# One low part ahead of the first row gather's index, one gate gathered two steps sooner, and each subtraction bound ahead of the next maxima

## The chip, the cores and the metric

The kernel runs on one core of a Trainium2 chip. The metric is the device time of one execution in microseconds (us); lower is better. Five engines work side by side, each on its own queue in order: TensorE (PE, with its weight loads shown apart as PEld), VectorE (DVE), ScalarE (ACT), GpSimd (POOL) and SyncE (SP, which here only issues transfers). They wait for each other through semaphores.

## What is computed

A linear attention over 8 batches, 8 heads, 576 positions and 64 channels, and behind it a mixture of 8 experts in which every token goes to its best expert alone:

```python
def phi(x):
    proj = np.einsum('bhsd,df->bhsf', x, w_phi)            # 64 -> 128 features
    proj = proj - np.max(np.abs(proj), axis=-1, keepdims=True)
    return np.concatenate([np.exp(proj), np.exp(-proj)], axis=-1)
q_p, k_p = phi(q), phi(k)
kv  = np.einsum('bhsf,bhsd->bhfd', k_p, v)
num = np.einsum('bhsf,bhfd->bhsd', q_p, kv)
den = np.einsum('bhsf,bhf->bhs', q_p, k_p.sum(2))[..., None] + 1e-6
x   = (num / den) as rows of 4608 tokens x 512
...
expert = argmax(x @ w_gate)                                # 8 experts
out[token] = gate[token] * (relu(x[token] @ w1[expert]) @ w2[expert])   # 512 -> 1024 -> 512
```

## The kernel before

**Attention.** It runs in 16 units of two batches and two heads. A unit's k and q are cut into pieces of one or two chunks of 128 positions (named by their first chunk: k8, k0, k2, ...). `project` multiplies a piece by w_phi into a PSUM tile `ps_proj` (two of them in turn), VectorE takes the maxima of the absolute values (L320) and subtracts them (L321, which is the last reader of `ps_proj`), ScalarE takes the two exponentials. Outside the first unit every fp32 factor is split in a high part (rounded copy, by ScalarE) and a low part (the rest, by VectorE or GpSimd), and a product is three matmuls. Then come the products with v (`pk`), a fold with w_gate, and the numerators (`pn`). The order of TensorE's work is written out by `half`, `PLAN_A` and `PLAN_B`; that of the other engines is set by a scheduler, except where `behind(m, other)` binds m after another instruction of its own engine, without a semaphore, or `paced(m, other)` makes m wait for an instruction of another engine. The first unit's loads and pieces stand in the string `ORDER`: `Lk2` loads part 2 of k, `VLt` the tail of v, `k4` projects piece 4.

**Routing.** Each token's place among its expert's tokens becomes a block of 128 rows. `tokens_of` multiplies selections into `pp`; VectorE turns it into `gidx`, the rows to gather for each block (L1030), `sidx`, the rows to write to, and `rows_f`. `experts_of` compares block numbers with the experts' bounds (`eg`, four instructions of L1065), GpSimd finishes `eg` (L1072, L1073) and VectorE sums it to `eidx`, the expert of each block (L1075), which SyncE reads to load weights.

**Experts.** Blocks are worked in 19 pairs, u = 0 to 18, and then one by one. Of each pair, `pair_first` makes the hidden layer (L1192 to L1194: products of high by high, low of x by high, high by low of the weights), ScalarE its relu's high part `hh` (L1199), VectorE the low part `hl` (L1200); `pair_second` multiplies by w2 (L1212 to L1214, of which L1214 needs `hl`). Both run over j = 0 to 3. `weights(u, k)` splits piece k of a pair's weights: `wh` by ScalarE (L1109), `wl` by VectorE (L1110). Pieces k = 4 to 7 are w2's. Pair 0's weights serve pair 1 too. `x_parts` turns the gathered rows `xg` of a block into `xh` and `xl` (with TensorE in pairs 0 and 1, L1173; later with VectorE, L1166). `write` scales a finished block by its gate on ScalarE (`ob`, L1267) and GpSimd scatters it (L1269).

Gathers run on GpSimd, in order: rows by `gidx` for block 3 (blocks 0 to 2 were gathered ahead), and from pair 2 on rows in quarters by `qidx`, eight to a pair; gates (`gate`) by `gather_gates`. The pair loop issues, at each j, a part of the quarters of pair u + 2, and at j = 3 the gates of pair u.

Of the kernel before, what the change touches and what calls it, by code (L numbers as in the profile page):

```python
# [9 lines left out]
F32 = mybir.dt.float32  # L10
# [4 lines left out]
ALU = mybir.AluOpType  # L15
# [41 lines left out]
def tile_linear_attention_moe(  # L57
# [144 lines left out]

    ORDER = "Lk0 Lk1 VLt Lk2 VL0 Lq0 k8 Lq1 Nk0 VL1 Lq2 Vt k0 V0 k2 C V1 k4 W"

# [83 lines left out]
    def chain(m):  # L288
# [3 lines left out]
        behind_order[0] = m  # L292

    def project(st, x, c0, n, link=lambda m: None):

# [16 lines left out]
        if st["u"] == 0 and (x, c0) == ("k", 4):  # L312
# [6 lines left out]
        psv = ps[:, 0:n].rearrange("p i h f -> p (i h) f")  # L319
        V.tensor_reduce(mx[:, 0 : 2 * n], psv, axis=AX.X, op=ALU.max, apply_absolute_value=True)  # L320
        V.tensor_tensor(  # L321
            t[:, 0 : 2 * n, :],
# [579 lines left out]
    def fetch_rows(out, source, index, rows):  # L902
        m = G.indirect_dma_start(  # L903
            out=out,
            out_offset=None,
            in_=source[0:rows],
            in_offset=bass.IndirectOffsetOnAxis(ap=index, axis=0),
            bounds_check=rows - 1,
            oob_is_err=False,
        )  # L910
        if lining[0]:
            lined(m)
        return m

# [83 lines left out]
    def block_of():  # L998
# [17 lines left out]
        for j0 in range(0, NTILE, 12):  # L1016
            V.tensor_tensor(
                bsel[:, j0 : j0 + 12, :],
                iota_p[:, 0:NB].unsqueeze(1).to_broadcast([P, 12, NB]),
                bi[:, j0 : j0 + 12].unsqueeze(2).to_broadcast([P, 12, NB]),  # L1020
                op=ALU.is_equal,
            )
# [33 lines left out]
    def experts_of():  # L1056
# [6 lines left out]
        for low, high, n0, n1 in places:  # L1063
            for j, edge in enumerate((low, high)):
# [5 lines left out]
                )  # L1070
                behind(m, st["places"])
        G.tensor_tensor(eg[:, 0], eg[:, 0], eg[:, 1], op=ALU.subtract)  # L1072
        st["experts"] = G.tensor_tensor(eg[:, 0], eg[:, 0], iota_e[0:1].unsqueeze(1).to_broadcast([1, NB, E]), op=ALU.mult)  # L1073
# [24 lines left out]
    def weights(u, k):  # L1098
# [12 lines left out]
        if (u, k) == (0, KD + 3):  # L1111
            behind(m, st["places"])
        for j in range(2) if u == 0 else [u]:
# [211 lines left out]
    tokens_of()  # L1325
    gather(1)
    weights(0, KD + 3)
    pair_second(0, 1)
# [17 lines left out]
    for u in range(1, NPAIR):  # L1346
# [5 lines left out]
        for j in range(4):  # L1352
            pair_first(u, j)
            for f in (parts[0], parts[2], parts[3], ())[j]:
                f(st["step"])
            if j == 3:
                for f in extra:
                    f(st["step"])
            if j in (1, 2):
# [116 lines left out]
```

## Time and profile before

| what | value |
|---|---|
| time, median of 3 runs | 868.35 us (868.28 to 869.65) |
| profiled execution, own time | 867.14 us |
| its span, first to last instruction | 865.3 us |
| granted TensorE clock, mean | 0.999 of full speed |
| busy share PE / PEld / DVE / ACT / POOL | 99 / 93 / 73 / 66 / 66 % |

The span is the part of the profiled execution in which instructions ran; 1.84 us of its own time lie outside. The profiled execution was 1.21 us shorter than the median of the runs. A matmul's end is modelled, so a short wait of TensorE shows fully only in its weight loads (PEld).

### The profile page before, as it was taken

How to read it: one execution, taken by the hardware profiler on the slowest of the kernel's cores; microseconds unless marked ns; L12 is line 12 of the kernel's file. 1: busy time of each engine (PE TensorE's matmuls, PEld its weight loads, DVE VectorE, ACT ScalarE, POOL GpSimd, SP SyncE). 2: the span in 40 equal slices, each digit the busy share in tenths (PEclk: the TensorE clock that was granted, in tenths of full speed). 3: DMA queues.
4: the chain of work that ended last, by engine and by line, in shares of the span. 5: the costliest groups of instructions: out<-in, count | busy, mean ns of one | idle time of the engine just before them, and what ended most of it. 6: DMA issues, size and time to landing. Idle time of an engine off the chain costs nothing. (4 is left out here: it accounts for less than half of the span.)

```text
span 865.3 us, 18092 instructions
## 1 busy us (share of the span) xinstructions
PE 855.6 (99%) x6589; PEld 803.8 (93%) x6589; DVE 634.9 (73%) x1049; ACT 570.9 (66%) x880; POOL 567.0 (66%) x419
## 2 busy tenths in 40 slices
PE   9999999999999999999999999999999999999997
PEld 7999999999999999999889999999999999999985
DVE  7678778887888788949768666666666777676672
ACT  6888888888778887753646555555555555555572
POOL 5667666876677767663887666666666666664772
PEclk9999999999999999999999999999999999999999
DMA  6233333523343334261154243541535644445651
GB/s 208 86 103 96 106 105 103 101 83 113 114 114 108 107 105 94 62 225 30 50 182 138 70 145 121 161 122 47 164 111 165 230 125 139 144 128 192 221 171 40
DMA packets 69884, 106.65 MB, mean 123 GB/s; under 512 B 13918, under 2 KB 31838, under 8 KB 69792
## 3 DMA queue, kind: packets, MB, share of 16 engines
q1 hardware_dynamic: 59312, 84.50, 32.7%
q0 software_dynamic: 9808, 20.81, 7.8%
q8 instruction: 53, 0.87, 0.4%
q14 instruction: 39, 0.32, 0.1%
q10 hardware_dynamic: 672, 0.15, 0.1%
HBM read 128.42 MB, written 20.26 MB: 172 GB/s over the span
## 5 line engine op out<-in xcount | busy, mean ns | idle before, releaser
L1110 DVE TENSOR_TENSOR wl<-raw,wh 128x1024 fp32r<-128x1024 f32 x160 | 201.5, 1270 | 91.1 <-ACT wh L1109 87.7
L903 POOL DMA_INDIRECT xg<-x_dram,qidx x148 | 174.4, 1179 | 76.2 <-ACT hh L1199 36.1
L1109 ACT CAST wh<-raw 128x1024 fp32r<-128x1024 f32 x168 | 174.4, 1047 | 40.0 <-PE po L1214 20.8
L490 PE MATMUL pn<-kf,qp 128*128 128x73 f32 (+1 forms) x1152 | 184.8, 255 | 0.0
L1194 PE MATMUL pm<-xh,wl 128*128 128x256 f32 x608 | 172.2, 283 | 0.0
L1193 PE MATMUL pm<-xl,wh 128*128 128x256 f32 x608 | 172.1, 283 | 0.0
L490 PEld LDWEIGHTS pn<-kf,qp 128*128 128x128 f32 x1152 | 171.4, 189 | 0.5
L1192 PE MATMUL pm<-xh,wh 128*128 128x256 f32 x608 | 171.6, 282 | 0.0
L355 POOL TENSOR_TENSOR kl<-e,kh 128x1024 fp32r<-128x1024 f32 x45 | 107.5, 2388 | 97.8 <-ACT kh L353 97.8
L320 DVE TENSOR_REDUCE mx<-ps_proj 128x4 f32<-128x512 f32 (+1 forms) x159 | 100.3, 632 | 49.3 <-PE ps_proj L310 48.2
L1213 PE MATMUL po<-wl,hh 128*128 128x512 f32 x304 | 119.3, 392 | 0.0
L1212 PE MATMUL po<-wh,hh 128*128 128x512 f32 x304 | 119.2, 393 | 0.0
L1214 PE MATMUL po<-wh,hl 128*128 128x512 f32 x304 | 118.3, 390 | 0.7 <-DVE hl L1200 0.7
L1192 PEld LDWEIGHTS pm<-xh,wh 128*128 128x128 f32 x608 | 116.4, 191 | 2.8
L1193 PEld LDWEIGHTS pm<-xl,wh 128*128 128x128 f32 x608 | 116.4, 191 | 2.8
L1194 PEld LDWEIGHTS pm<-xh,wl 128*128 128x128 f32 x608 | 116.4, 191 | 0.1
L321 DVE TENSOR_TENSOR t<-ps_proj,mx 128x512 f32<-128x512 f32 (+1 forms) x159 | 100.5, 634 | 4.4
L256 POOL TENSOR_TENSOR xl<-xr,xh 128x640 fp32r<-128x640 f32 (+1 forms) x60 | 96.8, 1630 | 9.4 <-ACT xh L255 8.8
L420 PE MATMUL pk<-kh,vl 128*64 128x256 f32 x300 | 101.1, 337 | 0.0
L420 PE MATMUL pk<-kl,vh 128*65 128x256 f32 x300 | 99.6, 332 | 0.0
L420 PE MATMUL pk<-kh,vh 128*65 128x256 f32 x300 | 99.2, 331 | 0.0
L903 POOL DMA_INDIRECT gate<-g_dram,gidx x41 | 58.2, 1418 | 54.8 <-ACT hh L1199 47.6
(223 smaller groups left out, 1889.4 us busy)
## 6 DMA issues: line engine op xcount, KB each, us to landing
raw<-w SPq DMA_DIRECT2D x168, 512.0 KB
vt<-vv SPq DMA_DIRECT2D x15, 640.0 KB
x_dram<-xrow SPq DMA_DIRECT2D x30, 256.0 KB
xr<-kT SPq DMA_DIRECT2D x15, 320.0 KB
xr<-qT SPq DMA_DIRECT2D x15, 320.0 KB
xr<-kT SPq DMA_DIRECT2D x17, 256.0 KB
xr<-qT SPq DMA_DIRECT2D x17, 256.0 KB
xg<-x_dram,qidx POOLq DMA_INDIRECT x148, 3.2
```

What stands on the lines that cost most here:

```text
L355: eng.tensor_tensor(kl, e[:, 0:m], kh, op=ALU.subtract)
L420: return T.matmul(st["pk", bb][0:n, hh, :], (vl if j == 1 else vh)[:, 2 * (c + (bb if c == 8 else 0)) + hh, 0:n], (kl if j == 2 else kh)[: ...
L490: m = T.matmul(pn[:, i - a, :] if c < 8 else pn[:, 2 + hh : 6 : 2, :], qp[:, s, s0 + hh, :], st["kf"][:, hh, s, c // 4, :] if c < 8 else s ...
L903: m = G.indirect_dma_start(out=out, out_offset=None, in_=source[0:rows], in_offset=bass.IndirectOffsetOnAxis(ap=index, axis=0), bounds_che ...
L1109: A.copy(th, raw[k])
L1110: m = (G if k in (POOL_LO0 if u == 0 else POOL_LO if u >= NPAIR else ()) else V).tensor_tensor(tl, raw[k], th, op=ALU.subtract)
L1192: T.matmul(pm[:, i], th, xh[:, k, :], start=(k == 0), stop=False)
L1193: T.matmul(pm[:, i], th, xl[:, k, :], start=False, stop=False)
L1194: T.matmul(pm[:, i], tl, xh[:, k, :], start=False, stop=(k == KD - 1))
L1212: T.matmul(po, hh[:, i, r], th[:, c], start=(i == j == 0), stop=False)
L1213: T.matmul(po, hh[:, i, r], tl[:, c], start=False, stop=False)
L1214: T.matmul(po, hl[:, i, r], th[:, c], start=False, stop=(i == 1 and j == 3))
```

## The change

Five edits:

- `ORDER`: the load of part 2 of k moves ahead of the load of v's tail (`Lk2` ahead of `VLt`).
- `project`: outside the first unit each L320 is bound behind the L321 of the piece before it.
- `weights(0, 7)`: its low part `wl`, bound behind the last instruction for `sidx` before, is bound behind `bsel`, which stands ahead of `gidx`.
- After `gather(1)` (the gather of block 3) GpSimd sets a tile `sent`, and the four `eg` instructions of VectorE wait for it.
- In pair 1 the gate (of block 3; the other is gathered already) is issued at j = 1 ahead of that step's quarters, not at j = 3. For other pairs nothing moves.

```diff
-    ORDER = "Lk0 Lk1 VLt Lk2 VL0 Lq0 k8 ..."
+    ORDER = "Lk0 Lk1 Lk2 VLt VL0 Lq0 k8 ..."
@@ project
-        V.tensor_reduce(mx[:, 0 : 2 * n], psv, axis=AX.X, op=ALU.max, apply_absolute_value=True)
-        V.tensor_tensor(
+        m = V.tensor_reduce(mx[:, 0 : 2 * n], psv, axis=AX.X, op=ALU.max, apply_absolute_value=True)
+        if shifted[0] is not None and st["u"] > 0:
+            behind(m, shifted[0])
+        shifted[0] = V.tensor_tensor(
@@ fetch_rows
+        st["fetch"] = m
@@ block_of
-            V.tensor_tensor(
+            st["bsel"] = V.tensor_tensor(
@@ experts_of
                 behind(m, st["places"])
+                paced(m, st["sent"])
@@ weights
         if (u, k) == (0, KD + 3):
-            behind(m, st["places"])
+            behind(m, st["bsel"])
@@
     gather(1)
+    st["sent"] = G.memset(sg.tile([1, 1], F32, name="sent"), 0.0)
+    behind(st["sent"], st["fetch"])
@@ pair loop
             pair_first(u, j)
+            if j == (1 if u == 1 else 3):
+                for f in extra:
+                    f(st["step"])
             for f in (parts[0], parts[2], parts[3], ())[j]:
                 f(st["step"])
-            if j == 3:
-                for f in extra:
-                    f(st["step"])
```

VectorE at a boundary between two units of the attention, before: the maxima (`mx`) and the subtraction (`t`) of a narrow piece, k8 (128x2 maxima, 128x256 elements), and of the wide piece behind it. The line numbers of the changed kernel are some lines higher.

```order
L355 TENSOR_TENSOR kl<-e,kh 128x1024
L320 TENSOR_REDUCE mx<-ps_proj 128x2
L320 TENSOR_REDUCE mx<-ps_proj 128x4
L321 TENSOR_TENSOR t<-ps_proj,mx 128x256
L321 TENSOR_TENSOR t<-ps_proj,mx 128x512
```

The same place on VectorE now:

```order
L359 TENSOR_TENSOR kl<-e,kh 128x1024
L322 TENSOR_REDUCE mx<-ps_proj 128x2
L325 TENSOR_TENSOR t<-ps_proj,mx 128x256
L322 TENSOR_REDUCE mx<-ps_proj 128x4
L325 TENSOR_TENSOR t<-ps_proj,mx 128x512
```

The narrow piece's subtraction now stands ahead of the wide piece's maxima. The two orders differ so at three unit boundaries and once at the end of the first unit; everywhere else they already stood as now.

VectorE around the index of block 3's gather, before (`wl` is the low part of `weights(0, 7)`; behind the last row, in both kernels, come the other three `eg`, `qidx`, an `xl`, `eidx`, and the `xl` of block 3):

```order
L1017 TENSOR_TENSOR bsel<-iota_p,bi 128x528 x3
L1030 TENSOR_SCALAR gidx<-pp 128x44
L1032 TENSOR_SCALAR emp<-pp 128x44
L1033 SCALAR_TENSOR_TENSOR sidx<-pp,emp 128x44
L1035 TENSOR_SCALAR rows_f<-pp 128x44
L1110 TENSOR_TENSOR wl<-raw_5836,wh 128x1024
L1065 TENSOR_TENSOR eg<-iota_p,first 1x304
```

The same place on VectorE now:

```order
L1022 TENSOR_TENSOR bsel<-iota_p,bi 128x528 x3
L1116 TENSOR_TENSOR wl<-raw_5836,wh 128x1024
L1035 TENSOR_SCALAR gidx<-pp 128x44
L1037 TENSOR_SCALAR emp<-pp 128x44
L1038 SCALAR_TENSOR_TENSOR sidx<-pp,emp 128x44
L1040 TENSOR_SCALAR rows_f<-pp 128x44
L1070 TENSOR_TENSOR eg<-iota_p,first 1x304
```

`wl` moved from behind the four instructions that read `pp` to ahead of them; the rest kept its order. On TensorE two products L1192 stood ahead of the first L1193 of pair 1 before, and one stands there now.

GpSimd from the end of routing into pairs 1 and 2, before (`out` is the scatter of a finished block; rows of quarters are run together):

```order
L1073 TENSOR_TENSOR eg<-eg,iota_p 1x352
L903 DMA xg<-x_dram,qidx 128x128 x8
L1269 DMA out<-ob,sidx_74 4608x512
L903 DMA xg<-x_dram,qidx 128x128 x2
L1269 DMA out<-ob,sidx_74 4608x512
L903 DMA xg<-x_dram,qidx 128x128 x6
L903 DMA gate<-g_dram,gidx 128x4
```

The same place on GpSimd now:

```order
L1079 TENSOR_TENSOR eg<-eg,iota_p 1x352
L907 DMA xg<-x_dram,qidx 128x128 x8
L1275 DMA out<-ob,sidx_74 4608x512
L907 DMA xg<-x_dram,qidx 128x128 x2
L1275 DMA out<-ob,sidx_74 4608x512
L907 DMA xg<-x_dram,qidx 128x128
L907 DMA gate<-g_dram,gidx 128x4
L907 DMA xg<-x_dram,qidx 128x128 x7
```

The gate passes five quarters; each of these five is sent one instruction later.

## Rows read from the trace of the kernel before

**Rows 1.** The page, part 1: busy us of each engine, share of the span, instructions.

```profile
PE 855.6 (99%) x6589; PEld 803.8 (93%) x6589; DVE 634.9 (73%) x1049; ACT 570.9 (66%) x880; POOL 567.0 (66%) x419
```

**Rows 2.** Busy time by stretch: the stretch and its length in us, busy us of each engine with its instructions, granted clock, DMA share, GB/s.

```profile
0.00:10.00 10.00, 8.84 (x34) 5.72 (x35) 6.55 (x20) 4.45 (x8) 4.66 (x22) 1.00 0.80 255
500.00:700.00 200.00, 200.00 (x1288) 182.75 (x1287) 136.08 (x143) 112.66 (x143) 124.95 (x107) 1.00 0.44 139
```

**Rows 3.** The waits of TensorE's weight loads: who waited, for whom, us in total, times, longest.

```profile
PEld px L1173 <- DMA xg<-x_dram,gidx: 1.8, 1, 1.8
PEld po L1214 <- DVE hl L1200: 1.2, 1, 1.2
PEld ps_proj L305 <- DMA xr<-kT: 0.9, 2, 0.7
```

**Rows 4.** The timeline of the first 9 us: start us, us, engine (SPq issues transfers), what, in brackets the idle time before and who ended it. The transfer at 2.21 is part 2 of k, that at 1.73 the tail of v; L305 projects, L407 copies v beside a column of ones, L432 is the first product with v.

```profile
1.73 0.44 SPq L400 DMA_DIRECT2D vt<-vv  x1
2.21 0.43 SPq L246 DMA_DIRECT2D xr<-kT  x1
6.42 0.73 PEld L305 LDWEIGHTS ps_proj<-w_bd,xr 128*128 128x128 f32 x4 [0.71 <-DMA xr<-kT]
5.39 0.40 POOL L407 COPY vf<-vt 128x256 f32<-128x256 f32 x1 [3.38 <-DMA vt<-vv]
7.39 0.59 PE L432 MATMUL pk<-ef,vf 128*65 128x256 f32 x2
```

**Rows 5.** The timeline at the three unit boundaries where TensorE's weight loads wait; VectorE and ScalarE at the first of them.

```profile
147.52 1.01 DVE L320 TENSOR_REDUCE mx<-ps_proj 128x2 f32<-128x256 f32 x2
148.45 1.01 DVE L321 TENSOR_TENSOR t<-ps_proj,mx 128x256 f32<-128x256 f32 x2
148.17 0.58 ACT L452 COPY kvT<-pk 65x512 f32<-65x512 f32 x1 [1.57 <-PE pk L420]
148.98 0.19 PEld L308 LDWEIGHTS ps_proj<-w_hi,xh 128*128 128x128 f32 x1 [0.23 <-ACT kvT L452]
243.40 0.19 PEld L308 LDWEIGHTS ps_proj<-w_hi,xh 128*128 128x128 f32 x1 [0.26 <-ACT kvT L452]
337.85 0.19 PEld L308 LDWEIGHTS ps_proj<-w_hi,xh 128*128 128x128 f32 x1 [0.27 <-ACT kvT L452]
```

**Rows 6.** The timeline around the gather of block 3 and the products that wait for it.

```profile
400.00 1.04 ACT L1109 CAST wh<-raw 128x1024 fp32r<-128x1024 f32 x1
407.94 1.95 DVE L1017 TENSOR_TENSOR bsel<-iota_p,bi 128x528 bf16<-128x528 f32 x3
410.73 0.20 DVE L1030 TENSOR_SCALAR gidx<-pp 128x44 int32<-128x44 f32 x1 [0.85 <-PE pp L1029]
411.31 1.22 DVE L1110 TENSOR_TENSOR wl<-raw,wh 128x1024 fp32r<-128x1024 f32 x1
411.45 2.00 POOL L903 DMA_INDIRECT xg<-x_dram,gidx  x1 [6.56 <-DVE rows_f L1035]
412.44 0.46 DVE L1065 TENSOR_TENSOR eg<-iota_p,first 1x304 f32<-1x304 f32 x1
415.57 0.51 DVE L1075 TENSOR_REDUCE eidx<-eg 1x44 int32<-1x352 f32 x1 [1.14 <-POOL eg L1073]
415.85 0.75 PE L1173 MATMUL px<-ident,xg 128*128 128x128 f32 x4 [1.41 <-DMA xg<-x_dram,gidx]
416.64 0.59 ACT L1174 CAST xh<-px 128x512 fp32r<-128x512 f32 x1 [2.96 <-PE px L1173]
417.25 0.69 DVE L1175 TENSOR_TENSOR xl<-px,xh 128x512 fp32r<-128x512 f32 x1 [1.18 <-ACT xh L1174]
417.82 0.40 PE L1192 MATMUL pm<-xh,wh 128*128 128x256 f32 x2
418.06 0.33 PE L1193 MATMUL pm<-xl,wh 128*128 128x256 f32 x1
```

**Rows 7.** Two other gathers on GpSimd: VectorE's work beside the one, GpSimd's next instruction behind the other.

```profile
427.85 3.49 DVE L1110 TENSOR_TENSOR wl<-raw,wh 128x1024 fp32r<-128x1024 f32 x3
430.28 1.98 POOL L903 DMA_INDIRECT xg<-x_dram,qidx  x1 [0.30 <-ACT hh L1199]
373.20 2.38 POOL L355 TENSOR_TENSOR kl<-e,kh 128x1024 fp32r<-128x1024 f32 x1
372.19 0.99 POOL L903 DMA_INDIRECT xg<-x_dram,gidx  x1 [0.30 <-issue]
```

**Rows 8.** The timeline around the gate of block 3, up to TensorE's wait for `hl`; the first row is the fourth quarter of pair 3's rows, the last the transpose of pair 3's second block.

```profile
437.01 1.00 POOL L903 DMA_INDIRECT xg<-x_dram,qidx  x1 [0.30 <-DVE wl L1110]
444.73 1.00 POOL L903 DMA_INDIRECT gate<-g_dram,gidx  x1 [0.30 <-issue]
448.40 0.69 ACT L1267 ACTIVATE ob<-po,gate 128x512 f32<-128x512 f32 x1 [4.97 <-DMA gate<-g_dram,gidx]
450.06 2.36 DVE L1110 TENSOR_TENSOR wl<-raw,wh 128x1024 fp32r<-128x1024 f32 x2 [7.38 <-ACT wh L1109]
452.33 0.68 DVE L1200 SCALAR_TENSOR_TENSOR hl<-pm,hh 128x512 fp32r<-128x512 f32 x1
453.07 0.50 PE L1214 MATMUL po<-wh,hl 128*128 128x512 f32 x1 [0.73 <-DVE hl L1200]
457.38 1.13 DVE L1166 STREAM_TRANSPOSE px<-xg 128x512 f32<-128x512 f32 x1
```

More of the change, by code (lines that the diff above doesn't have):

```diff
@@ L198, in raw_view @@
         return raw[k].rearrange("p (c f) -> p c f", c=2)
-    ORDER = "Lk0 Lk1 VLt Lk2 VL0 Lq0 k8 Lq1 Nk0 VL1 Lq2 Vt k0 V0 k2 C V1 k4 W"
+    ORDER = "Lk0 Lk1 Lk2 VLt VL0 Lq0 k8 Lq1 Nk0 VL1 Lq2 Vt k0 V0 k2 C V1 k4 W"
     V0 = {"t": (16, 20), "0": (0, 8), "1": (8, 16)}
@@ L292, in chain @@
         behind_order[0] = m
+    shifted = [None]
     def project(st, x, c0, n, link=lambda m: None):
```

## The prediction

> **What bounds the kernel now.** I read the busy time first: TensorE is busy for 855.6 of 865.3 us [rows 1], and from 500 to 700 us without a gap, at full granted clock [rows 2]. So the kernel ends when TensorE has done its list. An edit that takes work or waits from another engine gives nothing, unless TensorE waited for it, and then it gives what TensorE waited. Next I read the waits of TensorE's weight loads, since the ends of its products are modelled and hide short waits. There are few: 1.8 us for the gather of block 3, 1.2 for `hl`, 0.9 for transfers of k, 0.7 of it in one wait [rows 3], and three of 0.23 to 0.27 us that are put down to `kvT` [rows 5]. TensorE also waits at the very start and behind its last product, which the change does not touch. Last I read the timeline at each of these places, and set the five edits beside them. Each place has an edit, so the sum is over the places.
>
> **A. Part 2 of k ahead of v's tail.** SyncE issues v's tail at 1.73 and part 2 of k at 2.21 [rows 4]. The weight loads for piece 4 come at 6.42, after 0.71 idle that a transfer of k ended. Moved, that transfer is issued 0.48 us earlier, and 128 KB of v no longer lie ahead of it. In a stretch that moves 255 GB/s [rows 2] those would be 0.5 us. The gain is then about 0.5. It is bounded below by 0.3, where the transfer gains little, above by the whole wait, 0.71. The cover to watch is v's tail, which now comes later: its copy ran from 5.39 to 5.79, and the first product with v starts at 7.39 [rows 4], with 1.6 us between. In its new place the tail should have landed when part 2 of k had, at about 6.3. A copy of 0.40 ends at 6.7, against a product wanted at 6.9. I take **-0.5**.
>
> **B. Subtractions ahead of the next maxima.** TensorE's L308 projects into a `ps_proj` that the narrow piece's L321 must have read. At the first boundary both maxima run from 147.52 to 148.53, and only then the two subtractions, from 148.45 [rows 5]. The narrow one takes about 0.42 of these 1.01 us and ends at 148.87; the weight load goes at 148.98, 0.11 later. `kvT`, to which the profile gives the wait, had ended at 148.75, and a projection does not read it. Now the narrow subtraction follows the narrow maxima, which end at about 147.94. It ends at about 148.4, before TensorE wants the place at 148.75. The three waits, 0.23 + 0.26 + 0.27, go: **-0.75**. The wide piece's subtraction ends as before, since the same four instructions stand in the same stretch. The fourth place, at the end of the first unit, shows no wait: 0 by itself, but its earlier subtraction frees its `ps_proj` for a TensorE that A has made earlier.
>
> **C. `wl` ahead of `gidx`, and `sent`.** Before, `gidx` starts at 410.73, the gather at 411.45 (0.72 later), and it takes 2.00 us, until 413.45. The rows land 2.40 us behind that, when L1173 starts at 415.85 [rows 6]. VectorE was idle for 0.85 ahead of `gidx`, and `wl`'s `wh` is ScalarE's work of 400.00 to 401.04, so `wl` can start when `bsel` ends, at 409.89, and ends at 411.11. `gidx` goes from 410.73 to 411.11, a loss of 0.38, and the gather starts at 411.83. Does it still take 2.00? Another gather, started at 430.28 beside `wl` instructions that end at 431.34, ends at 432.26, 0.92 behind them; ours ended 0.92 behind its `wl` (412.53). One without `wl` beside it takes 0.99 [rows 7]. So I take 1.0: it ends at 412.83, 0.62 earlier, and the rows land at 415.23.
>
> [...]
>
> `sent` costs something. The `eg` instructions wait for a tile set behind the gather, so they start at about 413.0, not at 412.44: +0.56. From there to the end of `eidx` (416.08) are 3.64 us through GpSimd and back, so `eidx` ends at 416.64. Behind it on VectorE stands block 3's `xl`, which L1193 needs at 418.06. Its other input, `xh`, ends 0.62 earlier, at 416.61. `xl` so starts at 416.65 and not at 417.25, and L1193 at 417.46. Of these 0.60, 0.12 go back, as only one L1192 (0.12 each, 417.82 to 418.06 for two) fills the time ahead of it. Behind `eidx` also wait SyncE's weight loads and GpSimd's quarters for pair 2, 0.56 later. Pair 1 has yet to run, with 96 products of 0.12 and 48 of twice the columns, some 20 us by this estimate, so I cost that at nothing. `rows_f` comes 0.4 later to TensorE, ahead of the long wait that swallows it. L1193 comes 0.2 earlier if the gather takes 1.3, 0.5 if it takes 1.0: **-0.4**.
>
> **D. The gate of block 3.** ScalarE stood for 4.97 us until 448.40 for this gate, which GpSimd sent at 444.73, behind eight quarters [rows 8]. Behind it in ScalarE's queue were two `wh`, so VectorE stood 7.38 us, and then ran two `wl` (450.06 to 452.42) ahead of `hl`, which L1214 wanted. TensorE lost 0.73 by its products, 1.2 by its weight loads. Now the gate takes the turn of the fourth quarter, sent at 437.01. With C's 0.56 it goes at about 437.6 and, with the 3.7 us that the old one took (444.73 to 448.40), lands at 441.3. ScalarE wants it at 443.43. Even 3 us later the two `wl` would be done before `hl` is due. The five quarters it passes belong to pair 3 and go 1.3 us later (1.00 and 0.30 of issue). The last of them was sent before the gate, and VectorE's transpose of that block is at 457.38, without a wait, so I cost that at nothing. I take **-1.0**, between 0.73 and 1.2.
>
> **The sum.** 0.5 + 0.75 + 0.4 + 1.0 = 2.65 us, all of it waits of TensorE, with nothing else late in its list. Against the profiled execution's own 867.14 that is 864.5. That execution lay 1.21 under the median of the runs, 868.35, so for the median I forecast **865.7 us**, 0.3% faster.
>
> **The rivals.**
>
> 1. *v's tail lands late.* The copy of v then holds the first product with v, and A is lost: -2.15, 866.2 us. For it: the margin is only 0.2 us. Against: the same bytes are moved by the same moment as before.
> 2. *The gather keeps its 2.00 us.* It starts 0.38 later, ends at 413.83, and `eg` starts at 413.95. `eidx` ends at 417.6, `xl` at 418.3, L1193 comes at 418.4, and with the L1192 that is gone C is +0.46: -1.8, 866.55 us. Against: [rows 7].
> 3. *The boundary waits are for `kvT`, as the profile says.* B is nothing: -1.9, 866.45 us. Against: 0.23 us between its end and the weight load, where the subtraction's end fits to 0.11.
> 4. *The waits change place.* TensorE, earlier by each gain, runs into the next late thing (a load of k, weights that come by their own pace), and the end stays: 868.35 us. For it: behind every wait stands a second input that was not timed, as `eidx` in C. Against: 200 us on end in which TensorE never waits [rows 2].
> 5. *Slower: `sent` is set only when the gathered rows have landed.* Place: VectorE's queue ahead of `eidx`. The gather starts at 411.83; with the 4.40 us that it took to land, `eg` would start at 416.2, `xl` at 419.85, L1193 at 420.7, which is +2.6, or +2.7 with the L1192. Against -2.25 elsewhere the kernel is 0.45 slower, 868.8 us. It decides from a landing about 3.9 us behind the start, and each us more costs one. Against: behind a gather of 0.99 us GpSimd's next instruction started 0.02 later [rows 7].
>
> **How the numbers follow.** About 0.2%, 1.7 us, is what a measurement of this kernel can tell from no change. Chances: forecast 0.63, rivals 0.10, 0.10, 0.05, 0.08 and 0.04. The bounds of the terms add up to 1.98 to 3.17, or 866.4 to 865.2. The rest of the range is what executions differ by: one here lay 1.2 under the median, so I go down to 864.5. Upward it takes in rivals 1 to 3 with 0.7 for that spread, to 867.3. Faster by over 0.2% is below 866.6: nearly all of the forecast (0.60) and about six in ten of rivals 1 to 3 (0.15), together 0.75. Slower by over 0.2% is rival 5 with a late landing and what I have not thought of, 0.05; the rest, 0.20, is within.
>
> **What would show it.** A: the weight loads of piece 4 without a wait, at about 5.8. B: no wait of L308 at the three boundaries, each narrow subtraction right behind its maxima. C: a gather of about 1.0 us, the first L1173 wait at most 1.3 us. D: no `ob` held for a gate in pair 2's start, no wait of L1214. The forecast is wrong if one of these waits stays, if the first product with v waits for its copy, or if L1193 waits for `xl` behind `eidx` longer than before.

## The result: slower, by a stall that no term of the forecast held

The changed kernel takes **875.9 us** (median of 6 executions, 875.14 to 877.32) where the kernel before, run beside it, takes 868.56 (868.28 to 870.01): ratio 1.0083, 95% interval 1.007 to 1.0096. The forecast was 865.7, so the prediction was wrong in sign.

The profiled execution took 875.14 us, its span 873.1. The page after, busy time and granted clock in 40 slices of 21.8 us, against [rows 1]:

```profile
PE 860.1 (99%) x6589; PEld 806.4 (92%) x6589; DVE 635.6 (73%) x1049; ACT 570.9 (65%) x880; POOL 564.2 (65%) x420
PEclk9999999999999999999899999999999999999999
```

One slice has a lower clock, the twentieth. Busy time by stretch (columns as in [rows 2]):

```profile
400.00:420.00 20.00, 19.46 (x176) 16.77 (x175) 15.54 (x43) 6.29 (x9) 8.51 (x11) 1.00 0.09 22
420.00:440.00 20.00, 15.16 (x73) 12.07 (x72) 8.00 (x9) 8.10 (x10) 13.71 (x13) 0.83 0.20 60
440.00:460.00 20.00, 19.63 (x130) 17.84 (x129) 19.12 (x21) 13.45 (x18) 12.67 (x10) 1.00 0.60 188
500.00:700.00 200.00, 200.00 (x1279) 182.33 (x1278) 136.99 (x144) 110.87 (x142) 125.21 (x107) 1.00 0.45 141
```

The same stretch of the kernel before:

```profile
420.00:440.00 20.00, 20.00 (x137) 18.53 (x136) 19.34 (x21) 15.41 (x19) 16.34 (x13) 1.00 0.35 111
```

From 420 to 440 us, in pair 1, TensorE starts 73 products where it started 137, and VectorE and ScalarE do half of what they did. DMA is not the cause that meets the eye: its share is 0.20, less than before. Before and after that stretch the kernel runs as foreseen; from 500 to 700 TensorE is busy without a gap, as in [rows 2].

Since TensorE has the same 6589 products in both kernels, the n-th can be set beside the n-th. This table (worked out from the traces) gives by how many us a product starts later (+) or earlier (-) than in the kernel before, less that difference at the 20th product, at 7 us. The columns x2 to x16 are experiments below.

| product that starts before at | changed | x2: no C | x7: C without `sent` | x6: C without `wl` | x16: no gathers of pair 2 |
|---|---|---|---|---|---|
| 147.7 us (ahead of the first boundary) | +0.22 | -0.01 | 0.00 | +0.19 | +0.20 |
| 339.0 (behind the third) | -0.40 | -0.99 | -0.98 | -0.43 | -0.42 |
| 410.1 (ahead of C's place) | -0.29 | -0.94 | -0.93 | -0.33 | -0.33 |
| 421.6 (behind it) | -0.88 | -0.89 | -1.36 | -0.28 | -0.89 |
| 443.6 (ahead of D's place) | **+8.80** | -0.89 | -1.37 | -0.28 | -0.89 |
| 459.9 (behind it) | +7.80 | -1.89 | -2.36 | -1.28 | -1.88 |

So the edits gained most of what they were to gain (1.88 us in x16), and in the changed kernel about 9.7 us were lost between 421 and 444.

**The stall.** TensorE's waits there have no releaser; the profile puts them down to "issue" (the two largest groups; who waited, for whom, us in total, times, longest):

```profile
PE pm L1198 <- issue: 1.9, 2, 1.0
PE pm L1200 <- issue: 1.8, 3, 1.0
```

The timeline of the changed kernel there (L907 gathers, L1275 scatters, L1205 is `hh`, L1206 `hl`, L1116 `wl`; the rows of each engine by themselves, TensorE's last):

```profile
415.80 1.04 POOL L907 DMA_INDIRECT xg<-x_dram,qidx  x1 [0.16 <-issue]
...
419.75 1.03 POOL L907 DMA_INDIRECT xg<-x_dram,qidx  x1 [0.30 <-issue]
421.09 1.00 POOL L907 DMA_INDIRECT xg<-x_dram,qidx  x1 [0.30 <-issue]
...
431.60 1.03 POOL L907 DMA_INDIRECT xg<-x_dram,qidx  x1 [0.31 <-issue]
435.57 1.00 POOL L907 DMA_INDIRECT gate<-g_dram,gidx  x1 [2.94 <-ACT hh L1205]
...
422.09 0.60 ACT L1205 ACTIVATE hh<-pm 128x512 fp32r<-128x512 f32 x1 [2.50 <-remote]
434.39 0.60 ACT L1205 ACTIVATE hh<-pm 128x512 fp32r<-128x512 f32 x1 [9.81 <-remote]
...
419.82 1.22 DVE L1116 TENSOR_TENSOR wl<-raw,wh 128x1024 fp32r<-128x1024 f32 x1
435.02 0.69 DVE L1206 SCALAR_TENSOR_TENSOR hl<-pm,hh 128x512 fp32r<-128x512 f32 x1 [10.07 <-ACT hh L1205]
...
419.74 0.28 PE L1200 MATMUL pm<-xh,wl 128*128 128x256 f32 x1
428.50 0.28 PE L1200 MATMUL pm<-xh,wl 128*128 128x256 f32 x1 [1.01 <-issue]
```

GpSimd alone runs freely: thirteen indirect DMAs from 415.80 to 432.63, each about 1.0 us with 0.30 between. ScalarE's second `hh` waits 9.81 us for products that TensorE had started by 422.6; it goes at 434.39, 1.8 us behind the end of GpSimd's run. VectorE waits for that `hh`, and TensorE, which has work that waits for nobody, starts a product every 0.7 us or so instead of every 0.12. It stands idle for 4.84 of the 20 us, and from 431, behind the first of these gaps, to 437 it is granted a clock of 0.50 of full speed, where it has 1.00 up to 430 and from 438 on (0.83 over the stretch). The kernel before, at the same place of the program:

```profile
420.94 1.97 POOL L903 DMA_INDIRECT xg<-x_dram,qidx  x1 [0.31 <-issue]
423.22 1.50 POOL L903 DMA_INDIRECT xg<-x_dram,qidx  x1 [0.30 <-issue]
...
420.82 1.22 DVE L1110 TENSOR_TENSOR wl<-raw,wh 128x1024 fp32r<-128x1024 f32 x1
421.06 0.60 ACT L1199 ACTIVATE hh<-pm 128x512 fp32r<-128x512 f32 x1 [0.46 <-PE pm L1194]
```

There the fifth gather began 0.12 us *into* a `wl` and was stretched to 1.97, the next to 1.50, and no `hh` was late. In the changed kernel the edits have brought TensorE, ScalarE and VectorE 0.9 to 1.0 us forward in pair 1 (0.6 of it C's, by the table) but the quarters back by 0.11 (415.80, not 415.69): the fourth gather starts 0.07 us *ahead* of the `wl`, takes 1.03, and the fifth finds VectorE idle.

The lost stretch is not how the stall begins, though. The last product that the first `hh` needs starts at 419.74 and ends at 420.02. In x16, which has no stall, that `hh` follows this product's end by 0.04. Here it was due at about 420.06, with the fourth gather under way, and it came 2.0 late; the fifth gather began only at 421.09.

The places of the four edits in the changed kernel, in the order A, B, C, D (against [rows 4], [rows 5], [rows 6] and [rows 8]):

```profile
2.21 0.91 SPq L404 DMA_DIRECT2D vt<-vv  x2
6.42 0.73 PEld L307 LDWEIGHTS ps_proj<-w_bd,xr 128*128 128x128 f32 x4 [0.65 <-DMA xr<-kT]
6.89 0.40 POOL L411 COPY vf<-vt 128x256 f32<-128x256 f32 x1 [4.88 <-DMA vt<-vv]
7.34 0.19 PEld L436 LDWEIGHTS pk<-ef,vf 128*65 128x65 f32 x2 [0.20 <-POOL vf L411]
...
147.73 0.41 DVE L322 TENSOR_REDUCE mx<-ps_proj 128x2 f32<-128x256 f32 x1
148.17 0.42 DVE L325 TENSOR_TENSOR t<-ps_proj,mx 128x256 f32<-128x256 f32 x1
148.88 0.19 PEld L310 LDWEIGHTS ps_proj<-w_hi,xh 128*128 128x128 f32 x1
...
409.51 1.22 DVE L1116 TENSOR_TENSOR wl<-raw,wh 128x1024 fp32r<-128x1024 f32 x1
410.65 0.20 DVE L1035 TENSOR_SCALAR gidx<-pp 128x44 int32<-128x44 f32 x1
411.36 1.05 POOL L907 DMA_INDIRECT xg<-x_dram,gidx  x1 [6.75 <-DVE rows_f L1040]
412.53 0.47 DVE L1070 TENSOR_TENSOR eg<-iota_p,first 1x304 f32<-1x304 f32 x1 [1.24 <-POOL sent L1333]
414.85 0.75 PE L1179 MATMUL px<-ident,xg 128*128 128x128 f32 x4 [0.54 <-DMA xg<-x_dram,gidx]
417.00 0.19 PEld L1199 LDWEIGHTS pm<-xl,wh 128*128 128x128 f32 x1 [0.21 <-DVE xl L1181]
...
451.54 1.37 ACT L1273 ACTIVATE ob<-po,gate 128x512 f32<-128x512 f32 x2 [1.41 <-PE po L1220]
451.79 0.39 PE L1220 MATMUL po<-wh,hl 128*128 128x512 f32 x1
```

### The profile page after: what moved, and what is told of

Its sections match the earlier page's. It is cut to its first block, busy times and chain, and to the rows that moved or that the text cites. A ratio compares the mean times of both kernels' runs of the same rounds, so it can differ in the third digit from the quotient of the medians.

```text
span 873.1 us, 18093 instructions
## 1 busy us (share of the span) xinstructions
PE 860.1 (99%) x6589; PEld 806.4 (92%) x6589; DVE 635.6 (73%) x1049; ACT 570.9 (65%) x880; POOL 564.2 (65%) x420
## 5 line engine op out<-in xcount | busy, mean ns | idle before, releaser
L1116 DVE TENSOR_TENSOR wl<-raw,wh 128x1024 fp32r<-128x1024 f32 x160 | 201.3, 1270 | 73.5 <-ACT wh L1115 62.6
L907 POOL DMA_INDIRECT xg<-x_dram,qidx x148 | 171.6, 1159 | 84.9 <-ACT hh L1205 49.0
L1220 PE MATMUL po<-wh,hl 128*128 128x512 f32 x304 | 118.4, 390 | 0.0
L1205 ACT ACTIVATE hh<-pm 128x512 fp32r<-128x512 f32 x76 | 45.3, 596 | 77.7 <-PE pm L1200 59.8
```

Of the source, the lines that this page charges most:

```text
L907: m = G.indirect_dma_start(out=out, out_offset=None, in_=source[0:rows], in_offset=bass.IndirectOffsetOnAxis(ap=index, axis=0), bounds_che ...
L1116: m = (G if k in (POOL_LO0 if u == 0 else POOL_LO if u >= NPAIR else ()) else V).tensor_tensor(tl, raw[k], th, op=ALU.subtract)
L1220: T.matmul(po, hl[:, i, r], th[:, c], start=False, stop=(i == 1 and j == 3))
```

## The experiments

They ran in five sets: x1 to x4, x5 to x8, x9 to x12, x13 to x16, x17 and x18. Within a set all kernels, and the kernel before with them, ran on one chip, so kernels of one set are compared first. The kernel before's own executions lie within 3 us of each other in the second set and 7 to 9 us apart in the others.

| kernel | us, median (range, executions) | the kernel before beside it | ratio, 95% interval |
|---|---|---|---|
| x1: D undone | 877.1 (875.14 to 878.63, 10) | 870.74 (868.8 to 877.07, 31) | 1.0056, 1.0034 to 1.0077 |
| x2: C undone | 870.41 (865.79 to 873.81, 10) | the same | 0.9959, 0.9929 to 0.9989 |
| x3: A undone | 876.37 (875.67 to 877.76, 10) | the same | 1.0049, 1.0029 to 1.007 |
| x4: B undone | 877.53 (876.21 to 879.89, 10) | the same | 1.0053, 1.003 to 1.0077 |
| x5: two pauses | 866.67 (865.75 to 867.6, 8) | 867.61 (866.96 to 869.38, 19) | 0.9988, 0.9978 to 0.9999 |
| x6: `sent` alone of C | 867.09 (1) | the same | |
| x7: `wl` alone of C | 865.98 (1) | the same | |
| x8: pauses throughout | 866.11 (865.24 to 867.0, 10) | the same | 0.9981, 0.9972 to 0.9991 |
| x9: changed again | 875.42 (866.71 to 877.55, 10) | 869.84 (868.19 to 874.87, 31) | 1.0017, 0.9979 to 1.0054 |
| x10: x8 again | 871.77 (868.45 to 874.91, 10) | the same | 1.0007, 0.9984 to 1.0031 |
| x11: before, with pauses | 872.72 (870.33 to 874.61, 10) | the same | 1.0016, 0.9997 to 1.0035 |
| x12: x10, A undone | 869.91 (867.55 to 873.51, 10) | the same | 0.9988, 0.9962 to 1.0014 |
| x13: changed, third time | 876.29 (874.98 to 878.4, 10) | 871.63 (869.22 to 876.56, 26) | 1.0044, 1.0022 to 1.0066 |
| x14: x7 again | 873.93 (872.25 to 875.31, 10) | the same | 1.0018, 0.9997 to 1.0039 |
| x15: x6 again | 877.47 (875.49 to 879.16, 9) | the same | 1.0056, 1.0031 to 1.008 |
| x16: no gathers of pair 2 | 866.41 (865.95 to 868.46, 6) | the same | 0.9929, 0.9899 to 0.9958 |
| x17: gathers wait for `hh` | 871.88 (870.11 to 874.45, 12) | 870.28 (867.75 to 876.37, 23) | 1.0012, 0.9993 to 1.003 |
| x18: x17, C undone | 870.52 (867.88 to 871.57, 12) | the same | 0.9992, 0.9974 to 1.0011 |

### x1 to x4: which edit brings the stall

x1 puts block 3's gate back:

```diff
-            if j == (1 if u == 1 else 3):
-                for f in extra:
-                    f(st["step"])
             for f in (parts[0], parts[2], parts[3], ())[j]:
                 f(st["step"])
+            if j == 3:
+                for f in extra:
+                    f(st["step"])
```

> The changed kernel with edit D undone: block 3's gate goes behind the fourth step's quarters again. The changed kernel took 875.9 us, the kernel before 868.56. In its trace TensorE stands with no visible cause between 426 and 434 us and runs at half clock until 438, about 9.5 us in all. Theory G (the stall is GpSimd's: its gathers for pair 2 come one behind the other at 1.0 us each, because sent and wl shift them against VectorE): the gate stands behind that run, so the stall stays, and TensorE's wait for hl (about 1.0) comes back: 876 to 877. Theory K (the stall comes from the gate's new place among the quarters): the stall goes, 875.9 - 9.5 + 1.0 = 867.4.

x2 undoes C:

```diff
-                paced(m, st["sent"])
...
-            behind(m, st["bsel"])
+            behind(m, st["places"])
...
-    st["sent"] = G.memset(sg.tile([1, 1], F32, name="sent"), 0.0)
-    behind(st["sent"], st["fetch"])
```

> The changed kernel with edit C undone: wl stands behind places again and eg no longer waits for sent. Theory G: the first gather takes 2.0 us again, pair 2's gathers take their old places and are stretched by VectorE's wl now and then, and the stall goes: 875.9 - 9.5 + 1.0 (the wait for block 3's rows that C took) = 867.4. Theory K: the stall stays, 876 to 877.

x3 undoes A, `"Lk0 Lk1 VLt Lk2 ..."`:

> The changed kernel with edit A undone: v's tail ahead of part 2 of k. Its trace shows the weight loads of piece 4 at 6.42 us as before and a new wait of 0.2 us for v's copy, so A by itself should be worth between +0.2 and +0.4 us, a loss. Theories G and K: the stall stays, 875.5 to 876. If the time falls to about 866, the stall hangs on the moment at which pair 1 begins (theory P, a phase), not on an edit's place.

x4 undoes B:

```diff
-        if shifted[0] is not None and st["u"] > 0:
-            behind(m, shifted[0])
```

> The changed kernel with edit B undone: each subtraction where the scheduler puts it. The three waits of L310 at the unit boundaries, 0.23 to 0.27 us, come back, and everything behind them runs 0.7 us later. Theories G and K: the stall stays, 876.6. Theory P (a phase): another time by several us, 867 to 872.

With C every execution of x1, x3 and x4 takes 875 or more, and their traces have the stall in pair 1. Without C (x2) none takes over 873.81, the trace has no stall there, and the best executions, 865.79, 866.15 and 866.58, lie under every one of the kernel before. So it is C that brings the stall, not D (theory K falls), not A and not B. The kernel before is not free of late executions itself: 11 of its 31 in this set take over 874. The median of x2 came out 3 us above the 867.4 expected: its trace has smaller stalls later. In x1, TensorE's wait for `hl` did not come back: behind the stall `ob` waits only 0.39 for the old gate, and TensorE gains 0.99 at D's place without D.

The timeline of x2, first around the second `wl` of its pair 1, then at a small stall in a later pair:

```profile
419.83 2.02 POOL L907 DMA_INDIRECT xg<-x_dram,qidx  x1 [0.30 <-issue]
419.76 1.22 DVE L1115 TENSOR_TENSOR wl<-raw,wh 128x1024 fp32r<-128x1024 f32 x1
421.11 0.60 ACT L1204 ACTIVATE hh<-pm 128x512 fp32r<-128x512 f32 x1 [1.57 <-PE pm L1199]
...
627.10 1.04 POOL L907 DMA_INDIRECT xg<-x_dram,qidx  x1 [0.30 <-issue]
627.42 2.36 DVE L1115 TENSOR_TENSOR wl<-raw,wh 128x1024 fp32r<-128x1024 f32 x2 [3.79 <-issue]
633.99 0.39 PE L1218 MATMUL po<-wl,hh 128*128 128x512 f32 x1 [0.32 <-issue]
634.72 0.49 PE L1219 MATMUL po<-wh,hl 128*128 128x512 f32 x1 [0.34 <-issue]
634.80 1.05 ACT L1114 CAST wh<-raw 128x1024 fp32r<-128x1024 f32 x1 [2.75 <-PE pm L1199]
```

A gather that starts 0.07 us behind the start of a `wl` takes 2.02; in the changed kernel one that starts 0.07 ahead of it takes 1.03. The first `hh` of pair 1 is late here too, by 1.2 us, but no stall follows. At 627 us the gather is 0.32 ahead, eight gathers and scatters run unstretched (the longest 1.07), and ScalarE is held 2.75 us for products of TensorE. This suggested theory R of the next runs. All traces together, those of the later sets with them, bear it out for the later pairs: from 480 to 830 us they hold 214 runs of eight or more indirect DMAs without a pause. In 208 one of the first eight takes 1.2 us or more, and TensorE leaves 0.5 us or more between the starts of two products in or behind none of these. In six none does, and five of the six have such gaps, worth 0.4 to 1.0 us; the sixth is in x5, in the set without stalls. Ahead of 480 us the rule fails as it stands: in pair 1 of x1, x3, x4, x9, x13 and x15 the eighth DMA takes 1.48 to 1.64, and the stall is there; x2 and x17 have gaps at 473 us behind a run with a stretched gather early in it and eight or more unstretched ones after that.

### x5 to x8: pauses, and the halves of C

x5 gives GpSimd a pause of 0.55 us behind the fourth and the eighth quarter of pair 2, x8 behind every fourth gather, gates counted, up to the end of the pairs:

```diff
+        if st.get("pause"):
+            st["count"] = st.get("count", 0) + 1
+            if st["count"] % 4 == 0:
+                st["rest"] = G.memset(st["blank"], 0.0)
+                behind(st["rest"], m)
```

> The changed kernel with a pause in GpSimd's run of gathers: behind the fourth and the eighth quarter of pair 2 GpSimd sets a scratch tile of 128x512, some 0.6 us by its 128x512 copies. Theory R (the stall comes when eight or so indirect DMAs follow each other at 1.0 us and 0.30 of issue, with none of them stretched by VectorE: in the runs so far every pair with such a run has a stall of TensorE behind it, and no pair whose run holds one of 1.27 us or more): TensorE's waits for issue at 422 to 434 us go, half clock too, and the time is 875.9 - 9.5 = 866.4. Theory W (GpSimd's being busy without a gap is what holds the others up, whatever it does): GpSimd is as busy as before and the stall stays or grows: 876 to 878. Theory S (it is the wait for sent itself): it stays, 876.

> The changed kernel with wl behind places again; sent stays. The first gather is then stretched to 2.0 us by wl, and pair 2's quarters come about 0.9 us later than before the change (from 416.6), while TensorE and VectorE's wl at 419.7 to 422.0 stand where they stood. Theory R: what decides is whether one of the first eight quarters begins well inside a wl. The fourth would begin at 420.5, 0.3 before one ends, so it is stretched a little, to 1.2, and the stall is there in part: 869 to 875. Theory S: the stall is there in full, 876.

> The changed kernel without sent; wl stays ahead of gidx. The first gather takes 1.0 us, eg is not held, so eidx and the quarters come about 1.0 us earlier than in the changed kernel, from 414.8, and the wl stand where they stand there, at 418.7 to 421.0. Theory R: the quarters begin at 414.8, 416.1, 417.4, 418.7, 420.0; the one at 420.0 begins 0.14 into a wl that ends at 421.04 and is stretched to about 1.9, so no stall: 866 to 867. Theory S: no stall. If the stall stays, neither holds.

> The changed kernel with such a pause behind every fourth gather of rows from pair 2 on until the pairs end. Theory R: no stall anywhere in the pairs, neither the large one nor the small ones of 0.5 to 2.8 us that x2 shows at 474, 634 and 681 us: 865 to 866.5, and its runs lie within 2 us of each other where those of x2 lay 8 apart. Theory W: 876 or more.

x5, x7 and x8 came out as theory R had it; x6, for which it gave 869 to 875, took 867.09. The three would have come out so without it too: in this set no trace has the stall (x5 loses 0.9 us in pair 1, where its weight loads wait 0.78 for `hl`), and no execution is late, those of the kernel before included. x5's trace holds a run of eight unstretched DMAs at 554 us without a gap. What the set does give is the edits' worth without stalls (the table above), and a time: 866.1 to 866.7 for all five edits plus pauses, 865.98 for all but `sent`.

### x9 to x12: the changed kernel beside the pauses

x9 is the changed kernel itself. x11 is the kernel before with the pauses of x8, x12 is x8 with A undone.

> The changed kernel itself, once more, beside the kernel before and the three that follow on one chip. It took 875.9 us where the kernel before took 868.56; the runs with pauses were made on another chip, where the kernel before took 867.61. Theory R (a run of unstretched gathers): the stall is there again, 7 to 8.5 us slower than the kernel before. Theory H (the stall hangs on the chip; in the profile of x5 a run of eight unstretched gathers at 554 us passes without a stall): on a chip where the kernel before takes under 868 us the changed kernel takes 866 to 867.

> The kernel of x8, the changed one with a pause behind every fourth gather, on the same chip as x9. Theory R: 1.5 to 2.5 us faster than the kernel before and 8 to 10 faster than x9. Theory H: as x9 to within 1 us.

> The kernel before with the same pauses and none of the five edits. Theory R: its own runs of gathers hold stretched ones, so it loses next to nothing to stalls, and it comes within 0.5 us of the kernel before, unless that one's runs on this chip lie several us apart (as on the chip of x1 to x4, 868.8 to 877.1): then these are the small stalls, and it lies at the lower end of them.

> The kernel of x10 with edit A undone (v's tail ahead of part 2 of k). By the changed kernel's trace A gained nothing at the weight loads of piece 4 (6.42 us in both) and made a wait of 0.2 us for v's copy: the same as x10 to within 0.3 us. By the prediction's term it is 0.5 slower.

The changed kernel shows both faces in one set: 866.71, 867.34, 867.94 and 867.95 in four executions, 875.14 to 877.55 in six. So the stall is not certain, and without it the kernel is near where the edits put it. Theory H falls with that: the chip is by its number the one of x5 to x8, though the kernel before is slower on it now. So does the cure: x10 has a stall in spite of its pauses, 7.3 us from 422 to 444 by its products, where R said none. ScalarE in x10:

```profile
421.48 0.60 ACT L1214 ACTIVATE hh<-pm 128x512 fp32r<-128x512 f32 x1 [1.86 <-PE pm L1209]
429.53 0.60 ACT L1214 ACTIVATE hh<-pm 128x512 fp32r<-128x512 f32 x1 [5.57 <-remote]
```

A pause of 0.55 us behind every fourth gather does not keep the stall away. x11 was to come within 0.5 us of the kernel before, or at the lower end of its executions, and came 2.9 above its median. It lost its time elsewhere, 5.2 us between 450 and 460: there the old gate landed so late that ScalarE stood 7.34 us for it, against 4.97 in [rows 8]. x12 cannot be told from x10, so A has no worth that a measurement here can see.

### x13 to x16: are the gathers needed?

x14 and x15 are the kernels of x7 and x6. x16 replaces the eight gathers of pair 2 by memsets of the same length:

```diff
+        if b in blocks(2):
+            for _ in range(2):
+                m = G.memset(st["xg", b], 0.0)
+                behind(m, st["experts"])
+            return
         m = fetch_rows(st["xg", b][:, c, :], quarters, ...)
```

> The changed kernel, as the control for x14 to x16 on one chip. Its executions fall into two groups: with the stall 875 to 878, without it 866.5 to 868. Which share falls into which is not foreseen; where the kernel before takes 868 or less in all its executions, all of these should be in the lower group.

> The changed kernel without sent. If sent and what it delays by 0.56 us brings the stall: none or few of the executions above 872, where x13 has them. If wl ahead of gidx, and with it the first gather of 1.0 us, brings it: as x13. Without the stall 866 in any case (x7: 865.98).

> The changed kernel with wl behind places again, sent kept. If wl's place brings the stall: none or few executions above 872, where x13 has them. If sent brings it: as x13. Without the stall 867 (x6: 867.09).

> The changed kernel with the eight gathers of quarters for pair 2 replaced by sixteen memsets of a 128x512 tile on GpSimd, 0.55 us each by the pauses of x8, so that GpSimd is busy as long but moves nothing (pair 2's rows are left out and its blocks come out as zeros). If the gathers are needed for the stall: no execution above 870. If GpSimd's being busy, or the place in the program, is enough: as x13.

x16 answers the question. On a chip where the changed kernel takes 874.98 or more in all ten executions, x16 takes 866.41, 10 us less, and GpSimd is busy for 16.8 of the 20 us, not 13.7. Its stretch 420 to 440, and ScalarE's two `hh` in it:

```profile
420.00:440.00 20.00, 20.00 (x136) 18.52 (x135) 19.23 (x21) 14.21 (x18) 16.77 (x20) 1.00 0.24 75
```

```profile
420.83 0.60 ACT L1210 ACTIVATE hh<-pm 128x512 fp32r<-128x512 f32 x1 [0.46 <-PE pm L1205]
423.77 0.60 ACT L1210 ACTIVATE hh<-pm 128x512 fp32r<-128x512 f32 x1 [0.46 <-PE pm L1205]
```

Both halves of C bring the stall, each by itself: x15 loses 9.3 us between 422 and 444 by its products (its fourth gather starts 0.94 into a `wl` and is stretched to 1.15 only), x14 7.7, the changed kernel 9.7. In x14 the link to GpSimd is plainest. Its products for the first `hh` end at 419.3; ScalarE, then GpSimd, and behind them the eighth gather of x13, stretched in the midst of its stall:

```profile
425.23 0.60 ACT L1204 ACTIVATE hh<-pm 128x512 fp32r<-128x512 f32 x1 [6.33 <-remote]
...
424.29 1.02 POOL L1274 DMA_INDIRECT out<-ob,sidx  x1 [0.30 <-issue]
426.10 1.05 POOL L907 DMA_INDIRECT xg<-x_dram,qidx  x1 [0.78 <-issue]
...
424.51 1.58 POOL L907 DMA_INDIRECT xg<-x_dram,qidx  x1 [0.30 <-issue]
```

`hh` goes at 425.23, 0.08 ahead of the end of GpSimd's run of nine (425.31): its next gather is bound to wait for that very `hh`. Other traces do not fit so closely: in the changed kernel the first `hh` goes in the midst of the run and the second 1.8 us behind its end.

Set side by side, the first `hh` of pair 1 is at most 0.12 us late in the kernel before, x5 to x8 and x16, counted from 0.04 behind the end of its last product. In the other 14 traces it is late: by 0.96 to 1.81 in the three without C (x11, x2, x18), by 1.33 to 1.41 with C and pauses or stops (x12, x10, x17), by 2.0 to 5.9 in the rest. When it was due, only four or five of GpSimd's run of DMAs had begun. So something holds the products up ahead of any run of eight, with C and without; with C and without stops it goes on, in x2, x17 and x18 it does not.

### x17 and x18: stops instead of pauses

x17 makes GpSimd wait for ScalarE sooner; x18 is the same without C:

```diff
-    gather(2)
+    second = gather_steps(2)
+    for f in second[:4]:
+        f(None)
...
-            for f in (parts[0], parts[2], parts[3], ())[j]:
+            now = (second[4:], parts[0], parts[2], parts[3]) if u == 1 else (parts[0], parts[2], parts[3], ())
+            for f in now[j]:
                 f(st["step"])
```

> The changed kernel, in which the last four quarters of pair 2 wait for hh of pair 1's first step, and each later part of the quarters for the step behind the one it waited for. If the other engines are held up as long as GpSimd runs its indirect DMAs without a stop, the first hh comes at once where GpSimd stops (about 422 instead of 425 in x14), and the next stop comes six DMAs later at the latest, so the stall shrinks from 8 to 10 us to 3 at most: 866.5 without a stall, up to 870 with it. If stops do not help: as x13, 875 to 878, wherever the kernel before has executions above 870.

> x17 with edit C undone, so the edits A, B and D and the waits. By the prediction's terms it is 0.4 us slower than x17 (C). By the runs so far C is worth about nothing without a stall (x6 and x7 lie 1.1 apart, x5 and x8 between them) and brings the stall: 866 to 867 without one, and never later than x17 with it.

The profiled execution of x17 has no large stall in pair 1. Its GpSimd and ScalarE there:

```profile
421.42 1.02 POOL L1275 DMA_INDIRECT out<-ob,sidx  x1 [0.30 <-issue]
425.02 0.99 POOL L1275 DMA_INDIRECT out<-ob,sidx  x1 [2.58 <-ACT hh L1205]
...
421.81 0.60 ACT L1205 ACTIVATE hh<-pm 128x512 fp32r<-128x512 f32 x1 [1.88 <-PE pm L1200]
424.19 0.60 ACT L1205 ACTIVATE hh<-pm 128x512 fp32r<-128x512 f32 x1
```

The first `hh` is 1.4 late (its wait is 1.88, of which x16 has 0.46) and comes while GpSimd still runs a scatter; GpSimd then stops, the second `hh` waits for nothing, and TensorE loses 1.1 us up to 444, not 9.7. Its timed executions, 870.11 to 874.45, lie under all those of the changed kernel with a stall, though not in one set with them, and all above the 870 that was expected at most; what is left are small stalls further on (2.1 us at 475, 0.9 at 635). It is not faster than the kernel before, nor is x18 beyond its interval.

Where there are stalls, x2, the change without C, is 0.4% under the kernel before, and 6 to 7 us under x1, x3 and x4, which have C. In the set without stalls x8 is 0.2% under it; the changed kernel itself did not run in that set.

## Why the prediction was wrong

**What bounds the kernel: right.** TensorE waited for nothing outside the places named, and each wait taken away came back as time, until the stall.

**A, -0.5 forecast: nothing measurable.** Part 2 of k is issued 0.48 earlier, and the weight loads of piece 4 still start at 6.42, after 0.65 of waiting where it was 0.71. The step that failed is the one from issue to landing. Rival 1 came true too: v's copy runs at 6.89, not 5.39, and the first product with v waits 0.20. Over the traces the 20th product starts 0.49 earlier to 0.78 later than in the trace of before, with A as without it (x3 +0.77, x11 +0.72, x12 +0.06).

**B, -0.75 forecast: -0.98 in the kernels without `sent`,** 0.31 to 0.34 at each boundary (x2, x7, x14, x18), and 0.04 to 0.06 back later. The mechanism was right: the subtraction now follows its maxima, and the weight load goes at 148.88 without a wait. x4, without B, is 0.84 behind the changed kernel at the third boundary. Rival 3 falls.

**C, -0.4 forecast: -0.56 at its place,** -0.43 of it by `wl` alone (x7) and nothing by `sent` alone (x6). The gather takes 1.05, not 2.00, so rival 2 falls; `gidx` starts at 410.65, no later than before, though 0.2 later beside TensorE's products. `sent` was set at once, so rival 5 falls. But two costs of C were not seen. The small one: each kernel with `sent` loses some 0.55 us in the attention (x4 0.4), 0.16 to 0.22 between two boundaries, a little at a time, long before `sent` is set; none of the five without it does. The runs do not say why. The large one is the step "Behind `eidx` also wait SyncE's weight loads and GpSimd's quarters for pair 2 ... so I cost that at nothing". This is the step that failed: it priced the quarters' move by their lateness alone, for which pair 1's own work was cover enough, and left out what they would run beside. In its place the runs show the stall, 9.7 us of TensorE in the profiled execution. The rows were at hand to ask the question: [rows 7] had shown a gather of 1.98 us beside `wl` and one of 0.99 without, and I used that for one gather and did not ask which others would lose or gain a stretch. That the lost stretch is the cause is not shown.

**D, -1.0 forecast: -0.99,** against the kernel before; x1 cannot show it, as said. No `ob` waits for a gate, and L1220 does not wait for `hl`. The gate was sent at 435.57 even behind the stall.

**The sum.** Without the stall the trace of x16 gains 1.88 us on that of before from the 20th product to the end of the pairs: -0.98 + 0.55 - 0.56 - 0.99 is -1.98, and some 0.1 is given back between, against -2.65 forecast. What is missing is A and what `sent` costs. The four executions of x9 without the stall, 866.7 to 868.0, are what the forecast was about; one lies inside its range of 864.5 to 867.3, three above it. The stall, 9.7 us in the profiled execution, sits on top in the other 22 of the 26 timed ones. Rival 4, that waits change place, was not it either: the stall stands where TensorE had never waited. The chance of 0.05 for slower was for rival 5 "and what I have not thought of"; for an edit that shifts a run of thirteen DMAs against three engines that was too little.

**What is shown, and what stays open.** Shown, in the sets that have stalls: C brings the stall (x1 to x4), either half of C will do (x14, x15), and it is gone without the gathers of pair 2 (x16). From 480 us on, gaps of TensorE go with runs of indirect DMAs that nothing stretches (0 of 208 with a stretched one, 5 of 6 without). Argued only: what C does to pair 1. The lost stretch of the fifth gather could let the hold-up go on; it cannot begin it, since the first `hh` was late before. No run shifts the gathers by 0.1 us and nothing else, and a held VectorE has no `wl` beside the gathers (in the changed kernel it ran nothing from 424.95 to 435.02, and the six indirect DMAs begun in that time took 1.00 to 1.05), so unstretched runs may be an effect as well as a cause.

Open: what in the chip is held up. TensorE starts products, and the engine that needs them goes up to 9.8 us later. Open too is what the late executions of the kernel before are (over 874 in 11 of 31 beside x1 to x4, in 11 of 26 beside x13 to x16, with no trace of one), so C may make usual what happens there now and then; and why x5 to x8 had none on the chip of x9 to x12.

One rival stands untested: the recording of the profile. Behind 418 us the trace of the kernel before and those of x5 to x8 hold some 4,900 records of landed transfers, all others only 2,600 to 2,800, and stalls are in these others alone. x16 lacks such records and has no stall, so their loss is not enough for one; but it also leaves out the records of the very gathers it leaves out, and so cannot tell the gathers from their recording. No run here shows whether the recording holds an engine back, and all times here come from executions that were recorded.

## What to carry to other kernels

Between the changed kernel and x2, 0.14 us of one engine's queue against another's went with a gather of 1.03 us in the one (0.07 ahead of a `wl`) and of 2.02 in the other (0.07 behind it), so list for each moved chain (gathers above all) what it ran beside before and what after, and price both directions: a gather that is no longer slowed is an event too. Long runs of indirect DMAs on GpSimd went with stalls of the other engines in four of the five sets. Letting them wait for the consumers' progress every few is worth a trial: in x17 it went with 1.1 us lost in pair 1 instead of 9.7, though the kernel was no faster than before. And price each half of an edit by itself: `sent` gained nothing at its place and cost some 0.55 us in the attention, and its partner `wl` alone gave 0.43 of C's 0.56.

## What the runs showed of the hardware

- Whether a gather on GpSimd was stretched beside a `wl` of VectorE went with who started first: started 0.12 us (the kernel before) or 0.07 (x2) behind the `wl`, it took 1.97 and 2.02; started 0.07 ahead of it (the changed kernel), 1.03, and the `wl` its usual 1.22. At the border the starts in a trace do not tell: in the changed kernel a gather that starts 0.03 behind a `wl` (423.69, 423.66) takes 1.00, and the `wl` 1.29.
- In the changed kernel's trace, during an unbroken run of thirteen indirect DMAs on GpSimd, ScalarE waited up to 9.8 us for products long started, TensorE started one product in about 0.7 us, and the DMAs took their usual 1.0 us. With memsets in place of the first eight (x16) there was none of this; in the set of x5 to x8 runs of eight and more passed without it.
- The edit `sent`, whose tile of one element is first written at 412 us, went with some 0.55 us lost in the products of the first 340: in 14 traces with it, in none of the five others (x13 and x14 differ by it alone).
